# A state-space head and a long-convolution head in one kernel: parameter loads moved to another queue, and a new order of all operations

## The chip, the cores and the metric

The kernel runs on one core of a Trainium2 chip. The time is device microseconds of one launch, the median of the runs shown; the profile is one more execution, recorded by the hardware profiler. The engines are named as in the profile: PE (TensorE matmul) with PEld (its weight loads), DVE (VectorE), ACT (ScalarE), POOL (GpSimd) and SP (SyncE, which here only issues DMAs). Each engine works through its own queue in order.

## What is computed

Two independent heads over one sequence of 2048 positions with 640 channels in bf16; their outputs stand side by side.

```python
def _A_ref(x, Lambda_re, Lambda_im, B_re, B_im, C_re, C_im, log_dt, Dskip):
    Lam = Lambda_re + 1j * Lambda_im
    dt = jnp.exp(log_dt)
    Lam_bar = jnp.exp(dt * Lam)
    B_bar = ((Lam_bar - 1.0) / Lam)[:, None] * (B_re + 1j * B_im)
    Bu = jnp.einsum("bld,pd->blp", x + 0j, B_bar)
    for t in range(L):
        h = Lam_bar[None, :] * h + Bu[:, t, :]
    y = 2.0 * jnp.einsum("blp,dp->bld", hseq, C_re + 1j * C_im).real + x * Dskip
...
def _B_ref(q, k, v, shift_k, ssm_k, ssm_D):
    k_shift = sum over t of 4 taps: k_pad[:, t:t + S, :] * shift_k[:, ks - 1 - t]
    kv = k_shift * v
    y = irfft(rfft(kv, 2 * S) * rfft(ssm_k, 2 * S))[:S]   # per channel
    return q * (y + kv * ssm_D)
...
return jnp.concatenate([a, b], axis=-1)
```

Head A is a linear recurrence with 640 complex states, head B a causal convolution as long as the sequence.

## The kernel before

All operands live in one SBUF arena with named regions; PSUM's eight banks are handed out by number. `build` (line 1008) writes the whole program as a list of 806 operations. An operation has a number (its place in that list), a name, the engines that can do it with a planner's costs, a function that emits its instructions, and the regions that it reads and writes. `Program.depend` (92) derives from the regions which operations must come before which.

The order in which they are emitted, the engine of each and the PSUM bank of each matmul group are one string, `ORDER` (1112): `89V1` is operation 89 on DVE (V) with bank 1, and the other letters are A for ACT, G for POOL, T for PE, S for SP. A small `t` is a PE group whose matmuls are split into narrower pieces that run side by side in the array (`halves`, 585; `s1`, 877 to 883). `Program.emit` (122) walks the string and adds a wait for each dependence between engines. So the string alone sets the order on every engine's queue and the choice of engine where an operation has one: most evictions of PSUM can be done by DVE or ACT, many products of SBUF tiles by DVE or POOL. Where the eviction of a group is on ACT and the DVE form would multiply or add as well, ACT copies and a second operation (`em...`) does the product or sum; where it is on DVE that second one is empty. An `ad` (add) on ACT has PE add the old value through an identity matmul instead (695 to 699).

The stages, with the names that the text uses:

- Warm-ups (0 to 14, lines 513 to 525): matmuls on a zeroed tile while nothing else is there. `setup` and `tables_G` build index tables with iotas on POOL, integer products (`w_q` line 298, `g_q` line 337) and sines on ACT (303, 341).
- Parameters (83 to 147, `params`): three rows of Lambda and dt (84 to 86, line 355) are loaded into a zeroed tile, turned by one matmul (88 t_par, 363) and evicted (89 pv, 365); some thirty small DVE operations lead to the integer phases (105, 385), from there POOL makes multiples (110 fn1 to 114 ph, 393 to 397), ACT their sines (115 al_s, 401), DVE al (116, 403) and the rotation tiles rr (138 to 141, 443).
- B comes in three blocks: the first (154, 155, line 496, by ACT's queue) is turned by PE (156, 158 turn_B, 509) and evicted (157, 159, 511); the second and third (160 to 163, line 500) come by transposing DMAs. x comes in eight tiles (165 to 172 are x0 to x7, line 532), transposing too.
- up2, up1, up0 (198 to 257): B x for four groups of positions at a time, combined by rotations. up2 takes x4 to x7, up1 x2 and x3, up0a x0 and x1 (L566 and L588 to L596 in the profile; evictions L583, L616, L641). 208 up21_0 is the first of them, 220 up0a_0 the first that reads x0 and x1.
- coarse (304 to 324): the recurrence over 128 coarse steps as a scan on DVE, for two halves (307 cs_v0, 316 cs_v1; products L670 to L681). down (325 to 366) spreads it to all positions; project (713 to 805) applies C, adds x Dskip and stores.
- Head B: per block d of 128 channels, k and v are loaded by transposing DMAs (367, 368, 378, 379 and so on, line 815), four taps on DVE or ACT (cm, 837, shown as L205 or L206), sums and the product with v on DVE or POOL (841, 842), a round trip through DRAM (848, 858). All k blocks use one tile, so k1 (378) waits for the last tap of block 0 (374 cm0_0).
- The convolution by two-stage transforms: s1 (L877, L882, evictions L887) and s2 (L901, L914) forward for h (ssm_k) and k, products (pp, pq, py, pz, 925 to 932), r2 (L946, evictions er2 L951) and r1 (L967, er1 L985 or L983) back, for two halves of the channels. 177 addD0 (810) adds ssm_D to h before the first s1.

In the string before, the head of SP's queue is 148, 84, 85, 86, 171, 172, 160, 161, 169, 170, 367, and ACT's is 155, 154, 90.

Of the kernel before, what the change touches and what calls it, by code (L numbers as in the profile page):

```python
# [1092 lines left out]
def plain_order(P):  # L1093
# [16 lines left out]


ORDER = (
# [38 lines left out]
)  # L1151


# [68 lines left out]
```

## Time and profile before

| | us |
|---|---|
| runs shown | 192.4, 192.89, 192.89 |
| their median | 192.89 |
| the profiled execution, as a run | 194.15 |
| its span in the profile | 192.4 |
| PE busy | 179.8 (93%) |
| DVE busy | 162.9 (85%) |
| ACT busy | 141.1 (73%) |
| POOL busy | 73.8 (38%) |

The profile's instructions carry the line of kernel.py that emitted them; `128x1024` is partitions by elements. A queue's DMA issues stand under SPq or ACTq, with the time that the issuing took. The chain of waits is followed back from the last instruction; "issue" is time in which an engine waited for nothing that the profile shows. Operation numbers do not stand in the profile: they follow from the order on each engine.

### The profile page before, as it was taken

Reading aid. Unit: us, or ns where it says so; the run is one execution under the profiler, and the core shown is the slowest. Engines: PE = TensorE matmul, PEld = TensorE weight load, DVE = VectorE, ACT = ScalarE, POOL = GpSimd, SP = SyncE. Lnnn points to the kernel's source line nnn. Section 1 sums busy time; section 2 is a strip of 40 time slices with the busy share of each in tenths; the row PEclk is TensorE's granted clock in tenths of the full one; section 3 lists DMA queues with packets and bytes.
Section 4 is the critical chain, followed back from the end, with each engine's and each line's share of the span. In section 5 each row is a group of like instructions: output and inputs, shape, how many; then the busy total and the mean of one; then the engine's idle time right before and its main releaser. Section 6 shows DMA issues by size and latency. Waiting matters only on the chain.

```text
span 192.4 us, 7725 instructions
## 1 busy us (share of the span) xinstructions
PE 179.8 (93%) x3430; PEld 123.5 (64%) x3431; DVE 162.9 (85%) x226; ACT 141.1 (73%) x176; POOL 73.8 (38%) x60
## 2 busy tenths in 40 slices
PE   7879999999999999879997999999999999989991
PEld 2435555465668666657676766775879877777770
DVE  1837599999789598999989999999999999986841
ACT  2646979999999989999999699983579635581100
POOL 8199999700000000007100578529515020594300
PEclk9999999999999999999999999999999999999999
DMA  4999999999999999939998898209993726447585
GB/s 94 191 172 211 147 203 146 188 108 280 203 146 278 205 162 124 197 67 148 125 135 255 185 134 117 72 3 200 189 234 71 170 72 170 112 135 172 124 184 145
DMA packets 107883, 30.17 MB, mean 157 GB/s; under 512 B 102602, under 2 KB 107210, under 8 KB 107850
## 3 DMA queue, kind: packets, MB, share of 16 engines
q1 hardware_dynamic: 107562, 29.35, 89.5%
q8 instruction: 27, 0.44, 1.0%
q10 hardware_dynamic: 288, 0.33, 0.6%
q14 instruction: 6, 0.05, 0.1%
HBM read 10.99 MB, written 7.86 MB: 98 GB/s over the span
## 4 chain that ended last, share of the span: by engine, by line
PE 59%; DVE 22%; ACT 6%; DMA 5%; SPq 4%; issue 3%; DVEq 0%; ACTq 0%
PE acc L566 23%; PE acc L588 11%; PE acc L592 6%; PE acc L946 6%; PE acc L901 4%; PE acc L596 4%; DVE arena L716 4%; ACT arena L914 3%; DMA arena<-in_A_B_im_dram 2%; DVE arena L914 2%; DVE arena L887 2%; DMA arena<-in_A_Dskip_dram 2%; DVE arena L932 2%; PE acc L967 2%; SPq L532 2%
## 5 line engine op out<-in xcount | busy, mean ns | idle before, releaser
L566 PE MATMUL acc<-arena 128*64 128x512 bf16 x400 | 47.2, 388 | 1.0 <-DMA arena<-in_A_B_im_dram 1.0
L914 ACT CAST arena<-acc 128x960 bf16<-128x960 f32 (+1 forms) x36 | 31.8, 912 | 7.1 <-PE acc L901 6.7
L566 PEld LDWEIGHTS <-arena 128*64 128x64 bf16 x400 | 22.8, 108 | 21.9 <-issue 1.9
L887 ACT CAST arena<-acc 128x1024 bf16<-128x1024 f32 x36 | 34.8, 1068 | 1.4 <-PE acc L877 1.1
L588 PE MATMUL acc<-arena 128*128 128x320 bf16 (+3 forms) x241 | 33.8, 294 | 1.1 <-DVE arena L756 0.8
L588 PEld LDWEIGHTS <-arena 128*128 128x128 bf16 x242 | 21.8, 98 | 10.6 <-DVE arena L756 1.0
L592 PE MATMUL acc<-arena 128*64 128x320 bf16 (+2 forms) x318 | 27.1, 315 | 1.2 <-DVE arena L675 0.8
L901 PE MATMUL acc<-arena 128*64 128x160 bf16 x512 | 22.9, 234 | 0.8 <-ACT arena L914 0.2
L841 POOL TENSOR_TENSOR arena<-arena 128x2048 bf16<-128x2048 bf16 x1 | 4.1, 4066 | 50.7 <-DVE arena L205 50.7
L901 PEld LDWEIGHTS <-arena 128*64 128x64 bf16 x512 | 18.5, 110 | 5.1 <-ACT arena L914 2.2
L841 DVE TENSOR_TENSOR arena<-arena 128x2048 bf16<-128x2048 bf16 x14 | 20.0, 1430 | 2.0 <-ACT arena L206 1.8
L592 PEld LDWEIGHTS <-arena 128*64 128x64 bf16 x318 | 16.9, 110 | 6.3 <-ACT arena L887 1.2
L877 PE MATMUL acc<-arena 128*64 128x128 bf16 x464 | 15.9, 221 | 0.5 <-DVE arena L716 0.2
L951 ACT CAST arena<-acc 128x1024 bf16<-128x1024 f32 x15 | 14.6, 1022 | 2.0 <-PE acc L946 1.9
L877 PEld LDWEIGHTS <-arena 128*64 128x64 bf16 x464 | 13.7, 110 | 3.1 <-ACT arena L887 0.6
L928 POOL TENSOR_TENSOR arena<-arena 128x1280 bf16<-128x1280 bf16 x3 | 8.3, 2769 | 18.3 <-PE acc L877 16.0
L716 DVE TENSOR_TENSOR arena<-acc,arena 128x1024 bf16<-128x1024 f32 (+1 forms) x13 | 14.7, 1154 | 0.2
L205 DVE TENSOR_SCALAR arena<-arena 128x2048 bf16<-128x2048 bf16 (+1 forms) x17 | 13.3, 800 | 0.2
L762 POOL TENSOR_TENSOR arena<-arena 128x640 bf16<-128x640 f32 x3 | 4.4, 1450 | 21.3 <-ACT arena L754 21.3
L946 PE MATMUL acc<-arena 64*128 64x128 bf16 x320 | 11.3, 224 | 1.0 <-issue 0.5
L983 ACT CAST arena<-acc 128x960 bf16<-128x960 f32 (+1 forms) x6 | 4.8, 830 | 10.0 <-PE acc L967 10.0
L946 PEld LDWEIGHTS <-arena 64*128 64x128 bf16 x320 | 10.5, 144 | 2.3 <-issue 1.4
(141 smaller groups left out, 301.9 us busy)
## 6 DMA issues: line engine op xcount, KB each, us to landing
out_dram<-arena SPq DMA_DIRECT2D x31, 160.0 KB, 3.2
arena<-in_B_ssm_k_dram SPq DMA_DIRECT2D x8, 320.0 KB, 5.8
kv_rows<-arena SPq DMA_DIRECT2D x5, 512.0 KB, 3.5
arena<-kv_rows SPq DMA_DIRECT2D x16, 160.0 KB, 5.3
arena<-in_A_x_dram SPq DMA_DIRECT2D x16, 160.0 KB, 3.5
arena<-in_B_q_dram SPq DMA_DIRECT2D x8, 320.0 KB, 5.1
arena<-in_A_B_im_dram ACTq DMA_DIRECT2D x1, 160.0 KB, 2.4
arena<-in_A_B_re_dram ACTq DMA_DIRECT2D x1, 160.0 KB, 2.7
```

Source lines behind the costliest of these rows:

```text
L205: vm = lambda e: lambda out, in_, by: e.tensor_scalar_mul(out=out, in0=in_, scalar1=by)
L566: e.matmul(o[64 * r:64 * r + 64], lhsT=self.BT[j][:, r, d, :], rhs=self.XP[:, d, 2 * q:2 * q + 2], start=(d == 0), stop=(d == 4), skip_gro ...
L588: e.matmul(out, lhsT=lhsT, rhs=rhs, start=start, stop=stop, skip_group_check=True)
L592: e.matmul(out[cs], lhsT=lhsT[:, cs], rhs=rhs, start=start, stop=stop, skip_group_check=True, tile_position=(0, 64 * r))
L716: e.tensor_tensor(out=o, in0=b, in1=o, op=ALU.add)
L841: P.add(f"ca{d}_{j}", tt, lambda e: e.tensor_tensor(out=t1, in0=t1, in1=t2, op=ALU.add), outs=[t1], ins=[t1, t2])
L877: e.matmul(B[64 * b:64 * b + 64, 128 * i:128 * i + 128], lhsT=lh[i], rhs=F[:, b, :], start=True, stop=True, tile_position=(0, 64 * b))
L887: P.add(f"e1{what}{hf}_{u}", {PACT: act(1024), PDVE: dve(1024)}, lambda e, B: c.CP[e](out=out, in_=(B.rearrange("p (l n s k) -> p k s l n" ...
L901: e.matmul(B[64 * s:64 * s + 64, 512 * b + 160 * i:512 * b + 160 * i + 160], lhsT=c.W[:, k, 64 * b:64 * b + 64], rhs=self.AS[hf][:, k, 160 ...
L914: c.CP[e](out=out, in_=b.rearrange("p r (k j n) -> p r k j n", k=n, j=4) if nj > 1 else b.rearrange("p r (k x) -> p r k x", k=n))
L946: e.matmul(B[:, 512 * s + 128 * i:512 * s + 128 * i + 128], lhsT=lh[i][s][r], rhs=rh, start=(r == 0), stop=(r == 1), tile_position=(64 * s ...
L951: P.add(f"er2{hf}_{u}", {PACT: act(1024), PDVE: dve(1024)}, lambda e, B: c.CP[e](out=out, in_=B.rearrange("p (s n b) -> p b s n", s=2, n=4 ...
```

## The change

Only the string is replaced. Everything else, the list of operations with their code included, stays.

```diff
 ORDER = (
-    "148S0 118V0 143G0 83V0 29V0 155A0 0G0 6T6 84S0 7T6 11T4 4T5 30G0 109G0 1T0 16G0 15G0 49G0 58G0 154A0 85S0 86S0 17V0 149G0 88T1 "
-    "89V1 90A0 122V0 34G0 108G0 21G0 23V0 121V0 22V0 117V0 27V0 9T7 24V0 171S0 158T0 159A0 59V0 40V0 153V0 106G0 120V0 61V0 306V0 "
-    "26V0 75G0 107G0 10T7 156T6 91V0 60V0 172S0 92V0 95A0 98V0 65V0 99V0 62V0 67G0 100V0 123V0 42V0 13T7 101V0 41V0 25V0 157A6 "
...
-    "660V0 662V0 629V0 748G0 648V0 562T0 563A0 546T6 547A6 640V0 651V0 749S0 755S0 768S0 769V0 661V0 552T4 553A4 774S0 775V0 770T2 "
-    "771A2 776T6 777V6 675T4 676A4 667T2 668V2 679T0 680A0 683T6 684V6 673T4 674A4 685T2 551G0 558S0 561S0 778G0 766G0 772G0 686A2 "
...
+    "0G0 1T7 143G0 120V0 14T1 30G0 2T4 107G0 16G0 154A0 13T5 6T6 155A0 21G0 119V0 108G0 15G0 83V0 85A0 17V0 12T7 22V0 65V0 67G0 "
+    "24V0 71G0 66V0 86A0 156T4 157V4 10T5 7T1 84A0 11T0 158T5 159A5 4T1 88T2 8T6 89V2 90A0 91V0 92V0 98V0 26V0 118V0 23V0 99V0 27V0 "
+    "100V0 5T4 46G0 95A0 96A0 34G0 36V0 68G0 72G0 148S0 93A0 152A0 172S0 101V0 25V0 9T2 3T0 58G0 59V0 122V0 40V0 60V0 43V0 20A0 "
+    "41V0 42V0 35V0 121V0 102V0 32V0 37V0 123V0 103V0 44V0 61V0 18V0 104V0 28V0 171S0 208T5 209A5 45V0 160S0 117V0 105V0 110G0 "
...
+    "661V0 629V0 550A6 764T2 546T4 547A4 545G0 551G0 659V0 651V0 749S0 755S0 768S0 559S0 774S0 560S0 552T6 553A6 662V0 763V0 640V0 "
+    "775V0 770T0 769V0 771A0 765V2 766V0 776T6 777V6 778G0 561S0 675T4 676A4 772G0 667T2 679T0 680A0 683T6 564V0 668V2 673T4 548G0 "
+    "684V6 767S0 674A4 685T2 686A2 558S0 773S0 779S0 671T0 672V0 786S0 677T6 681T4 800S0 669T2 670V2 554G0 568S0 758T0 757V0 759V0 "
...
 )
```

Read by queue, this gives:

| queue | before | after |
|---|---|---|
| SP, head | 148, 84, 85, 86, x6, x7, 160, 161, x4, x5, k0 | 148, x7, x6, 160, 161, x5, x4, k0 |
| SP, x0 and x1 | v0, k1, x0, x1, v1, pl0 | v0, k1, v1, x1, x0, 260 |
| ACT, head | 155, 154, 90 | 154, 155, 85, 86, 84, 159, 90 |
| PE, head | 5 warm-up groups, 88, 9, 158, 10, 156, 7 groups, 208 | 6 groups, 156, 10, 7, 11, 158, 4, 88, 8, 5, 9, 3, 208 |
| POOL, first table products (68, 72) | after 110 to 112 | before 110 |

ScalarE gives to DVE 132, 134, 157, 199, 205, 219, 255, 265, 332, 348, 467, 544, 563, 670 and 747, and takes from it 135, 207, 209, 213, 247, 249, 374, 471, 550, 556, 590, 644, 655, 678 and 688. DVE gives to POOL 484, 486, 495, 545, 729, 760, 781, 784, 787 and 801, and takes from it 485, 487, 498, 557, 564, 627, 689, 705, 751, 766 and 795 (some of the `em` among these are empty on either side). Of the PE groups in narrow pieces, 33 before, 30 are left, 11 of them new.

64 rows, old and new, of the table ORDER are left out of this document.

## Prediction

> **What bounds the kernel now.** I read the page first, then the busy time in stretches cut where the chain of waits changes engine, then that chain in order of time, then the instructions of the head, of the x loads and of the last stage.
>
> ```profile
> span 192.4 us, 7725 instructions
> PE 179.8 (93%) x3430; PEld 123.5 (64%) x3431; DVE 162.9 (85%) x226; ACT 141.1 (73%) x176; POOL 73.8 (38%) x60
> DMA  4999999999999999939998898209993726447585
> ...
> 12.50:38.40 25.90, 25.90 (x232) 13.78 (x233) 20.69 (x16) 21.47 (x21) 24.59 (x17) 1.00 1.27 178
> 38.40:66.90 28.50, 28.50 (x606) 18.94 (x606) 24.81 (x33) 27.75 (x40) 0.00 (x0) 1.00 1.09 202
> 66.90:165.80 98.90, 93.94 (x2033) 69.92 (x2032) 94.70 (x110) 79.27 (x96) 30.81 (x12) 1.00 0.87 142
> 165.80:188.40 22.60, 21.95 (x516) 17.20 (x516) 16.20 (x21) 7.22 (x8) 11.01 (x7) 1.00 0.59 147
> ```
>
> The columns after the window are its length and the busy time of PE, PEld, DVE, ACT and POOL; the last three are granted clock, share of the DMA engines and GB/s. From 12.5 to 66.9 us PE has no gap at all, and from 38.4 on ACT is nearly as full. From 66.9 to 165.8 DVE is the fullest engine (94.70 of 98.90 us). From 165.8 on PE sets the end again. So no stage has slack to give: the time ahead of 12.5 and the small waits after 66.9 can be won, all else can only be lost.
>
> ```profile
> 1.24 0.49 SPq L355
> ...
> 2.49 1.44 SPq L532
> ...
> 3.98 1.83 SPq L532
> ...
> 5.85 1.79 SPq L500
> ...
> 7.68 4.69 DMA arena<-in_A_B_im_dram
> ...
> 12.50 22.81 PE acc L566 x200
> ```
>
> This is the start of the chain: the three parameter rows (L355) stand ahead of x's tiles 6 and 7 (L532) and of the second block of B (L500) on SP's queue, and PE's steady stream starts when that block lands. The granted clock is 1.00 in every stretch and does not enter.
>
> **The change, part by part.** Every edit is in the order string: the same 806 operations, 3 DMAs moved from SP to ScalarE, 15 evictions and scalings moved from ScalarE to DVE and 15 back, 10 from DVE to POOL and 11 back, and all queues permuted.
>
> *SP's queue.* It loses the three L355 issues: x7 starts at 1.24 where x6 started at 2.49, so what follows is 1.25 us earlier, and the imaginary part of B's block lands at 6.43 + 4.69 = 11.1 instead of 12.4. ScalarE issues the three rows behind its own two loads while it has nothing else to do.
>
> ```profile
> 1.28 3.59 PE L524 MATMUL acc<-arena 128*128 128x512 bf16 x8 [1.28 <-POOL arena L520]
> 5.18 0.17 PE L363 MATMUL acc<-arena 128*128 128x30 bf16 x1 [0.31 <-DMA arena<-in_A_log_dt_dram]
> 5.21 0.38 PE L524 MATMUL acc<-arena 128*128 128x512 bf16 x1
> 5.42 0.44 PE L509 MATMUL acc<-arena 128*128 128x128 bf16 x5
> 6.20 1.47 PE L524 MATMUL acc<-arena 128*128 128x512 bf16 x6
> 9.03 2.45 PE L566 MATMUL acc<-arena 128*64 128x512 bf16 x20
> 9.32 0.17 DVE L385 CAST arena<-arena 128x10 int32<-128x10 f32 x1
> ```
>
> *PE's head.* The first real group (208, up21_0) does not follow x alone: it stands behind the warm-ups. The new queue has nine warm-up matmuls, turn_B, three, turn_B, two, the parameter turn (88), then six. By the rows, with 1.47 / 6 for each later one: 1.28 + 3.59 + 0.38 + 0.44 + 0.74 + 0.44 + 0.49 + 0.17 + 1.47 = 9.0, as now (9.03). It ends at 11.5, when B's block is there, so the second group starts at 11.5 instead of 12.5: **a gain of 1.0 us**, as a start.
>
> The parameter turn goes from 5.18 to 7.4. Behind it DVE has 34 operations up to the phase integers (105, L385); its operations there follow each other by about 0.11 us now, which gives 12 instead of 9.3. POOL's list behind these up to ph (114) I estimate at 9.3 us, so al_s on ScalarE can run from 21.3; ScalarE's own queue reaches it at about 23, after the first evictions and two taps of the k convolution. These 1.7 us cover the delay. If the cover goes, the evictions 201, 215 and 217 right behind al_s are late next, and with them PE's banks.
>
> *The x tiles that come late.* In the new queue x1 and x0 (166, 165) stand behind k1 and v1 (378, 379); now they go between them. And k1 waits for cm0_0 (374), which moves from DVE to ScalarE.
>
> ```profile
> 32.86 2.21 DVE L205 TENSOR_SCALAR arena<-arena 128x2048 bf16<-128x2048 bf16 x1
> 35.10 2.03 SPq L815 DMA_TRANSPOSE arena<-in_B_k_dram  x1
> 37.17 3.25 SPq L532 DMA_TRANSPOSE arena<-in_A_x_dram  x2
> 40.47 4.00 SPq L815 DMA_TRANSPOSE arena<-in_B_v_dram  x1
> ...
> DMA to landing us min/median/max: 3.8/4.8/6.4
> ...
> 49.80 2.43 PE L566 MATMUL acc<-arena 128*64 128x512 bf16 x20
> ```
>
> On ScalarE cm0_0 stands behind the eviction of the last up2 group (207). PE ends that at 11.5 + 9 x 2.28 = 32.0 (22.81 / 10 is the pace of twenty L566 matmuls); behind two table sines that stand ahead of it I put 207's end at 34.2 and cm0_0's, at some 2 us, at 36.2. So k1 goes out at 36.3, v1 at 38.4, x1 at 42.4, x0 at about 44.1 (half of 3.25 for one). The last row but one is the time from issue to landing of the eight x loads. With the median x0 lands at 48.9, with the longest at 50.5. The group that reads both (220, up0a_0) starts at 49.8 now, and would at 48.8 with the gain. I take 6.4, because x1 and x0 stand behind two larger transposes and the DMA engines are full in those slices: 220 at 50.5, so the gain of 1.0 is lost and **0.7 us** with it. Bounds: from 0.9 gained (x0 at 48.9) to 2.0 lost (1.3 us more, for a landing behind v1's data).
>
> *PE from there to cs_v0* (307, now at the end of its gapless stretch) has the same groups, but one s1 group fewer (180 goes ahead of 220) and another no longer split in quarters (192): **-0.15**. ScalarE's list has, by the sum of its rows, 0.7 us more ahead of cs_v0; the 4.4 us that it idles from 12.5 to 38.4 leave room for that.
>
> *DVE's stage.*
>
> ```profile
> 67.41 0.82 DVE L670 TENSOR_TENSOR arena<-acc,arena 128x640 bf16<-128x640 f32 x1 [2.32 <-PE acc L588]
> 74.53 0.42 DVE L641 CAST arena<-acc 128x256 bf16<-128x256 f32 x1 [0.60 <-PE acc L596]
> ...
> L716 DVE TENSOR_TENSOR arena<-acc,arena 128x1024 bf16<-128x1024 f32 x12 | 14.2, 1215 | 0.2
> L928 DVE TENSOR_TENSOR arena<-arena 128x1280 bf16<-128x1280 bf16 x13 | 10.5, 828 | 0.1
> L914 DVE CAST arena<-acc 128x960 bf16<-128x960 f32 x8 | 9.2, 1154 | 0.8 <-PE acc L901 0.4
> L756 DVE TENSOR_TENSOR arena<-acc,arena 128x640 bf16<-128x640 f32 x11 | 8.9, 820 | 2.5 <-PE acc L588 2.0
> ```
>
> DVE waits 2.32 us for cs_v0, so this stage moves with PE. Between cs_v1_m (317) and the last product of the second half 13 operations leave DVE's list and 14 come in. By these means (0.82 us for 640 columns from PSUM or a quarter product, 1.15 for 960, 1.22 for 1024, about 0.45 for the small ones) both sum to 10.8: **0**, bounds 0.7 either way. The wait of 0.60 goes, since its eviction (247) moves to ScalarE; another may come for cs_v1, whose eviction (249) moves too: **-0.3**, between -0.6 and 0.
>
> *The last r2 stage.*
>
> ```profile
> 164.88 0.82 DVE L930 TENSOR_TENSOR arena<-arena 128x1280 bf16<-128x1280 bf16 x1
> 165.62 0.49 DVE L725 TENSOR_TENSOR arena<-arena 128x640 bf16<-128x640 bf16 x1
> 166.24 0.82 DVE L756 TENSOR_TENSOR arena<-acc,arena 128x640 bf16<-128x640 f32 x1
> 167.16 2.35 DVE L951 CAST arena<-acc 128x1024 bf16<-128x1024 f32 x2
> 170.48 2.36 DVE L951 CAST arena<-acc 128x1024 bf16<-128x1024 f32 x2 [0.96 <-PE acc L946]
> 171.79 2.89 PE L588 MATMUL acc<-arena 128*128 128x320 bf16 x20
> ```
>
> Now the last product ends at 165.7 and er21_8 at 169.5, 3.8 us later. The new list puts xd10 (0.4) and ev_C9 (0.8) in between, which now stand ahead; with the overlap of starts that makes 4.8 us. The groups r21_5, r21_7 and r21_1 follow er21_8's bank (1.6 us at their pace), then C8: 6.4 us behind the last product instead of 6.1. **+0.35**; bounds 0 (PE's own pace hides it) to 1.3 (nothing does). Behind C8 the same groups run to the end.
>
> *Sum.* -1.0 + 1.7 - 0.15 - 0.3 + 0.35 = +0.6. The profiled execution took 194.15 us as a run, of which the span is 192.4; all terms are differences within that span, and the median of the runs shown is 192.89, so the forecast is 192.89 + 0.6 = **193.5 us**. About 0.3% (0.58 us) is what a measurement of this kernel can tell from no change.
>
> **The rivals.**
>
> *The head gain stays.* x0 lands by the median: -0.9, -0.15, -0.6, +0.35, together -1.3: 191.6. For it: SP stands idle for some 4 us ahead of k1 in the new queue, so the DMA engines may have emptied. Against it: 6.4 us was needed by loads in this same stretch.
>
> *POOL holds DVE's adds.*
>
> ```profile
> 16.43 2.08 POOL L298 TENSOR_TENSOR arena<-arena 128x1024 int32<-128x1024 int32 x1
> 16.68 1.93 DVE L403 TENSOR_TENSOR arena<-arena 128x80 f32<-128x80 f32 x1
> ```
>
> An 80-column product on DVE took 1.93 us and ended as POOL's table product did. The new list runs two such POOL products (68, 72) at 5 to 9 us, where POOL idles now and DVE has its small parameter operations: up to one product, 1.9 us, which is 0.2 more than al_s's cover. Later POOL's last product (80) can meet addD (177), for which PE waits at 37.5 with nothing before it, and k1's chain moves as well: 193.5 + 0.9 (half a product on average) = 194.4. It decides once POOL's list ends later than 36 us. The Trainium skill, SBUF — State Buffer, Who interferes with whom, says that a DVE instruction with two SBUF inputs and a GpSimd instruction that reads SBUF exclude each other for the whole instruction, which would hold the small products at 7 to 9 us too; no row here shows that at their size.
>
> *Nothing in sum.* The string may not do what it says for the time: PE's head is set by its warm-ups, not by x, and gain, late x and tail cancel to 192.9.
>
> **How the numbers follow.** Forecast 0.39 (own range 193.0 to 194.3), head gain kept 0.33, POOL and later waits 0.15, nothing 0.13. Of the forecast's share 0.32 is slower by over 0.3% and 0.07 within; with 0.14 of POOL's this is slower 0.46, faster 0.34, same 0.20. The range goes from 0.3 under the kept gain, 191.3, to the 2.0 us loss of the x term instead of 0.7 net with the whole tail, 192.89 + 2.0 - 0.15 - 0.3 + 1.3 = 195.7.
>
> **What would show it.** Right: the second up2 group at 11.5; the parameter turn near 7.4; k1 issued after 36; a wait of L566 for x up to about 50.5; cs_v0 near 67.4; more than 4.5 us from the last product to er21_8. Wrong: up0a_0 near 48.9 without a wait (then the time is near 191.6), addD waiting on POOL with s1h0 behind it, or a new gap of over 1 us in DVE between 70 and 165, which none of the terms has.

## The result, and the profile after

The changed kernel is a little faster: its median is 192.38 us (20 runs, 190.55 to 194.75) beside 193.30 us for the kernel before (20 runs, 191.72 to 194.62), a ratio of 0.9933 with a 95% interval of 0.9912 to 0.9955. Two later comparisons of the same two kernels gave 0.9959 [0.9929, 0.9989] and 0.9928 [0.9895, 0.9961]. Over all of its runs the kernel after has a median of 192.36 (44 runs), the kernel before 193.31 (170 runs): 0.95 us. The forecast was 193.5, slower. (A median here is over all runs of a kernel; a ratio leaves out the runs that took over 1.5% more than the kernel's fastest, so the two can differ by some tenths of a per cent.)

The profiled execution took 193.28 us as a run, with a span of 191.5. The page of the kernel after, and the busy time in the stretches of the prediction (length, PE, PEld, DVE, ACT, POOL, granted clock, DMA share, GB/s):

```profile
span 191.5 us, 7710 instructions
PE 181.0 (94%) x3425; PEld 123.9 (65%) x3425; DVE 157.3 (82%) x226; ACT 143.5 (75%) x176; POOL 71.9 (38%) x60
```

```profile
12.50:38.40 25.90, 25.80 (x286) 13.94 (x282) 15.47 (x14) 23.72 (x24) 22.39 (x20) 1.00 1.17 157
38.40:66.90 28.50, 27.12 (x530) 18.21 (x526) 23.28 (x32) 26.61 (x36) 0.00 (x0) 1.00 1.09 194
66.90:165.80 98.90, 94.43 (x2043) 69.27 (x2040) 96.09 (x114) 80.02 (x97) 28.70 (x11) 1.00 0.82 145
165.80:188.40 22.60, 22.41 (x521) 17.41 (x518) 15.47 (x19) 8.88 (x10) 12.31 (x8) 1.00 0.67 167
```

The bounds are the same ones: PE to 66.9 us, DVE to 165.8, PE to the end. New is a hole in PE between 38.4 and 66.9 (27.12 of 28.50 where the kernel before had 28.50). The start of the chain of waits and PE's and SP's timelines of the kernel after show the head and that hole:

```profile
3.04 1.83 SPq L532
4.92 1.79 SPq L500
6.75 1.75 SPq L500
```

```profile
7.08 0.18 PE L363 MATMUL acc<-arena 128*128 128x30 bf16 x1
...
8.50 2.45 PE L566 MATMUL acc<-arena 128*64 128x512 bf16 x20
11.25 2.04 PE L566 MATMUL acc<-arena 128*64 128x512 bf16 x16 [0.30 <-DMA arena<-in_A_B_im_dram]
...
50.98 2.47 PE L566 MATMUL acc<-arena 128*64 128x512 bf16 x20 [1.34 <-ACT arena L341]
```

```profile
36.07 2.13 SPq L815 DMA_TRANSPOSE arena<-in_B_k_dram  x1
38.25 3.38 SPq L815 DMA_TRANSPOSE arena<-in_B_v_dram  x1
41.67 3.37 SPq L532 DMA_TRANSPOSE arena<-in_A_x_dram  x2
```

The second up2 group starts at 11.2 instead of 12.5, the parameter turn (L363) stands at 7.1, k1 goes out at 36.07, and up0a_0 waits 1.34 us. The view puts that wait down to a sine on ACT (L341), but this group does not read it. Of the two x loads of the last row the view of line 532 says:

```profile
L532 SPq DMA_TRANSPOSE arena<-in_A_x_dram x2: 1407/1664/1922, 41.7 to 43.1; - x2
...
DMA to landing us min/median/max: 4.5/6.1/7.7
```

x0, issued at 43.12, took the longest of these: it landed at 50.85, and the group started 0.1 us later. In another execution of the same kernel (the run e15 below) ACT's sines stand where they stood, PE starts before they end, and x0 took 5.3 us:

```profile
48.48 2.22 ACT L341 ACTIVATE arena<-arena 128x1024 bf16<-128x1024 int32 x2
...
49.45 2.48 PE L566 MATMUL acc<-arena 128*64 128x512 bf16 x20
```

```profile
DMA to landing us min/median/max: 4.5/4.9/5.3
```

So every sign that the prediction named for being right is in the first profile (cs_v0 at 67.77, and 4.87 us from the last product to er21_8), and still the kernel is faster. Here and below a PE group starts with its first weight load, up to 0.25 us ahead of its first matmul. C0 to C15 are the groups of project, `st_A0` to `st_A15` their stores; s2k0_19, s1h1_3 and r10_16 are single groups of s2, s1 and r1. PE's last group, C13, starts only 0.1 us earlier than before (186.55 against 186.65); the other 0.8 us of the spans' difference lies behind it, where nothing but stores runs. SP's queue at the end, before and after:

```profile
179.96 0.35 SPq L766 DMA_DIRECT2D out_dram<-arena  x1
180.69 0.35 SPq L740 DMA_DIRECT2D out_dram<-arena  x1
181.13 1.66 SPq L724 DMA_DIRECT2D arena<-in_A_x_dram  x1
182.84 4.72 SPq L1001 DMA_DIRECT2D out_dram<-arena  x6
187.66 1.02 SPq L766 DMA_DIRECT2D out_dram<-arena  x2
188.86 0.33 SPq L740 DMA_DIRECT2D out_dram<-arena  x1
```

```profile
178.57 0.34 SPq L724 DMA_DIRECT2D arena<-in_A_x_dram  x1
179.01 3.33 SPq L1001 DMA_DIRECT2D out_dram<-arena  x4
182.39 0.49 SPq L766 DMA_DIRECT2D out_dram<-arena  x1
...
187.81 0.35 SPq L766 DMA_DIRECT2D out_dram<-arena  x1
188.77 0.35 SPq L740 DMA_DIRECT2D out_dram<-arena  x1
```

Before, two of part B's first four stores of the second half (L1001) stand behind st_A15 and st_A13, which wait for their evictions, and behind a load that takes 1.66 us to issue; six stores of 160 KB then go out in one row. After, all four go out at 179.0. The windows of before and of after (the last two columns are DMA share and GB/s):

```profile
180.00:184.00 4.00, 4.00 (x149) 3.16 (x149) 2.77 (x4) 0.69 (x1) 1.39 (x1) 1.00 0.57 146
...
188.00:193.00 5.00, 0.30 (x3) 0.00 (x0) 0.49 (x1) 0.00 (x0) 0.00 (x0) 0.98 0.47 122
```

```profile
180.00:184.00 4.00, 4.00 (x120) 2.93 (x118) 3.53 (x5) 0.96 (x1) 1.40 (x1) 1.00 0.88 197
...
188.00:193.00 5.00, 0.21 (x2) 0.00 (x0) 0.49 (x1) 0.00 (x0) 0.00 (x0) 0.74 0.34 91
```

The DMA engines are half idle where the kernel after uses them, and that work is still in flight at the end: the last store lands 2.62 us after its issue before and 1.78 after.

One execution of a kernel differs from the next by up to 1 us in its parts, so the account below is made from all profiles of the runs that follow, stage by stage, between starts of PE groups that have the same work ahead of them in both orders (the median, in brackets the range and the number of executions that run this stage in that order, single moved operations aside; e2, which its waits put 7 us back, is left out behind cs_v0):

| stage, us | old order | new order | forecast |
|---|---|---|---|
| start to the third up2 group (up21_4) | 14.46 (14.14 to 14.64, 7) | 13.57 (13.25 to 14.03, 12) | -1.0 |
| from there to cs_v0 | 52.34 (52.30 to 52.77, 7) | 52.84 (52.42 to 54.43, 8) | +1.55 |
| the same, x0 and x1 between k1 and v1 | | 52.46 (52.45 to 52.62, 3) | |
| cs_v0 to C8 | 104.34 (103.67 to 104.94, 4) | 103.99 (103.70 to 106.06, 12) | +0.05 |
| of it, r10_16 to C8 | 12.55 (12.33 to 12.91, 5) | 11.90 (11.89 to 12.04, 11) | +0.35 |
| C8 to C13, PE's last group | 14.86 (14.86 to 15.07, 6) | 14.86 (13) | 0 |
| C13 to the end | 5.72 (5.18 to 6.03, 5) | 5.26 (4.76 to 6.73, 12) | 0 |

The medians' differences add up to -0.9 + 0.5 - 0.35 - 0.5 = -1.25, the means' to -0.8 + 0.65 + 0 - 0.3 = -0.45; the times say -0.95.

### The profile page after: what moved, and what is told of

The parts are those of the page before. It is cut to its first block, busy times and chain, and to the rows that moved or that the text cites. A ratio compares the mean times of both kernels' runs of the same rounds, so it can differ in the third digit from the quotient of the medians.

```text
span 191.5 us, 7710 instructions
## 1 busy us (share of the span) xinstructions
PE 181.0 (94%) x3425; PEld 123.9 (65%) x3425; DVE 157.3 (82%) x226; ACT 143.5 (75%) x176; POOL 71.9 (38%) x60
## 4 chain that ended last, share of the span: by engine, by line
PE 55%; ACT 18%; DVE 11%; SPq 6%; issue 5%; DMA 4%; ACTq 0%; DVEq 0%
PE acc L588 17%; PE acc L566 12%; PE acc L901 6%; PE acc L946 6%; ACT arena L887 5%; PE acc L592 4%; DMA arena<-in_B_k_dram 4%; DVE arena L716 4%; SPq L532 4%; ACT arena L914 3%; PE acc L877 3%; ACT arena L206 3%; PE acc L967 3%; PE acc L596 3%; ACT arena L341 2%
## 5 line engine op out<-in xcount | busy, mean ns | idle before, releaser
L588 PE MATMUL acc<-arena 128*128 128x320 bf16 (+3 forms) x290 | 42.1, 299 | 0.2 <-issue 0.2
L914 ACT CAST arena<-acc 128x960 bf16<-128x960 f32 (+1 forms) x39 | 34.0, 902 | 7.7 <-PE acc L901 7.3
L566 PEld LDWEIGHTS <-arena 128*64 128x64 bf16 x400 | 23.7, 108 | 22.3 <-issue 1.7
L588 PEld LDWEIGHTS <-arena 128*128 128x128 bf16 x290 | 26.3, 98 | 12.4 <-ACT arena L914 0.8
L841 POOL TENSOR_TENSOR arena<-arena 128x2048 bf16<-128x2048 bf16 x1 | 4.1, 4075 | 53.5 <-DVE arena L205 53.5
L901 PEld LDWEIGHTS <-arena 128*64 128x64 bf16 x512 | 18.2, 109 | 6.0 <-ACT arena L914 3.1
L841 DVE TENSOR_TENSOR arena<-arena 128x2048 bf16<-128x2048 bf16 x14 | 17.8, 1275 | 3.6 <-ACT arena L206 3.5
L592 PE MATMUL acc<-arena 128*64 128x320 bf16 (+2 forms) x216 | 18.6, 312 | 0.9 <-DVE arena L675 0.6
L716 DVE TENSOR_TENSOR arena<-acc,arena 128x1024 bf16<-128x1024 f32 (+1 forms) x15 | 16.1, 1109 | 0.1
L877 PEld LDWEIGHTS <-arena 128*64 128x64 bf16 x416 | 12.7, 110 | 4.2 <-ACT arena L887 2.0
L205 DVE TENSOR_SCALAR arena<-arena 128x2048 bf16<-128x2048 bf16 (+1 forms) x17 | 11.3, 680 | 4.5 <-DMA arena<-in_B_k_dram 4.3
L983 ACT CAST arena<-acc 128x960 bf16<-128x960 f32 (+1 forms) x7 | 5.8, 845 | 11.8 <-PE acc L967 9.9
L592 PEld LDWEIGHTS <-arena 128*64 128x64 bf16 x216 | 11.5, 110 | 4.2 <-ACT arena L887 1.0
L756 DVE TENSOR_TENSOR arena<-acc,arena 128x640 bf16<-128x640 f32 x12 | 9.8, 820 | 4.2 <-PE acc L588 3.5
L990 POOL TENSOR_TENSOR arena<-arena 128x960 bf16<-128x960 bf16 (+1 forms) x5 | 8.8, 1769 | 11.4 <-ACT arena L983 11.4
L946 PE MATMUL acc<-arena 64*128 64x128 bf16 x320 | 11.2, 225 | 0.3 <-DVE arena L756 0.3
```

The lines of the kernel that those rows point to most:

```text
L205: vm = lambda e: lambda out, in_, by: e.tensor_scalar_mul(out=out, in0=in_, scalar1=by)
L566: e.matmul(o[64 * r:64 * r + 64], lhsT=self.BT[j][:, r, d, :], rhs=self.XP[:, d, 2 * q:2 * q + 2], start=(d == 0), stop=(d == 4), skip_gro ...
L588: e.matmul(out, lhsT=lhsT, rhs=rhs, start=start, stop=stop, skip_group_check=True)
L592: e.matmul(out[cs], lhsT=lhsT[:, cs], rhs=rhs, start=start, stop=stop, skip_group_check=True, tile_position=(0, 64 * r))
L716: e.tensor_tensor(out=o, in0=b, in1=o, op=ALU.add)
L841: P.add(f"ca{d}_{j}", tt, lambda e: e.tensor_tensor(out=t1, in0=t1, in1=t2, op=ALU.add), outs=[t1], ins=[t1, t2])
```

## The experiments

All edits are in the order string unless said otherwise. In the diffs, `SP:` is a part of SP's queue. Medians with the number of runs, and the ratio to the kernel before on the same chip.

**Three splices.** Because both strings hold the same 806 operations, a head of one can be followed by the rest of the other.

e1, the new head:

```diff
-old[0:806]
+new[0:300] + what is left, as in old
```

> The new order up to and with cs_v0 (its first 300 operations), the old order for the rest. Theory A (the new head loses time because x's tiles 1 and 0 come late, and what was won lies behind the head): PE waits about 1.3 us for x ahead of up0a_0, cs_v0 starts 0.9 us later than before (near 67.8), and that reaches the end: 193.3 + 0.9 = 194.2. Rival B (the head's earlier start is what the end shows): 192.4. Rival C (the old middle takes up what the head loses, since DVE sets the end there): 193.3.

193.94 (12), 1.0026 [0.9995, 1.0056]. cs_v0 at 66.27, with 0.41 us of waiting ahead of up0a_0: the head does not lose the 0.9 of theory A. But from cs_v0 to s2k0_19, 87 us into the kernel, it takes 20.90 us where both whole orders take 19.9: the seam costs 1.0.

e2, the new middle:

```diff
-old[0:806]
+old[0:301] + new up to 700 operations + what is left, as in old
```

> The old order up to cs_v0, the new one for the operations between (some 400, to about 165 us), the old one from there. Theory A: the middle gives back what the head loses, so alone it makes the kernel some 0.9 us faster: 192.4. Rival B: the middle is neutral: 193.3. Rival C (moved evictions put waits on DVE that the new head covers): 194.

199.81 (6), 1.0347 [1.0304, 1.0390]: no theory. From cs_v0 to s2k0_19 it takes 23.1 us where both whole orders take 19.9, and at the other end C10 waits for C9's eviction, which the new order has behind the last product, while the old order gives C10 the same bank:

```profile
165.99 1.25 PE L588 MATMUL acc<-arena 128*128 128x320 bf16 x4 [2.69 <-DVE arena L756]
```

e3, the new tail:

```diff
-old[0:806]
+old[0:700] + what is left, as in new
```

> The old order up to about 165 us, the new one for its last 106 operations. Theory A (the last stores of the new order reach SP's queue sooner, so that the last one has fewer transfers in flight beside it): the last product (C13) ends where it did, within 0.4 us, and the last store lands under 2 us after its issue instead of 2.6: 193.3 - 0.8 = 192.5. Rival B (the end of the profiled executions differs by chance): 193.3, the last store as before. Rival C (the wait for er21_8 behind the last product is paid at the end): 193.6.

194.37 (12), 1.0070 [1.0039, 1.0102], over all three theories. At its seam PE waits 1.23 us ahead of r10_22, and the last store needs 2.7 us. None of the three splices can be read as a part of the change: each seam brings a wait of 1 us or more that neither order has.

**Where x's tiles 0 and 1 stand.** e4 issues them ahead of k1, e6 between k1 and v1 as the kernel before does, all else as after; e12 and e16 are repeats of e6, e5 and e15 of the kernel after.

```diff
-SP: 368 378 379 166 165 260
+SP: 368 166 165 378 379 260      (e4)
+SP: 368 378 165 166 379 260      (e6, e12, e16)
```

> The kernel after, with x's tiles 1 and 0 issued ahead of k1 and v1 instead of behind them. Theory A: x0 lands before 45, the 1.34 us ahead of up0a_0 go, cs_v0 starts near 66.5; all carried to the end this is 192.4 - 1.3 = 191.1. Rival B (the stage of DVE behind it takes up what PE wins, since the k and v transfers are now 3 us later): cs_v0 early, but the time within 0.4 of 192.4. Rival C (k1 at 39 instead of 36 delays the gated product, and DVE waits for it): slower than 192.8.

194.13 (12), 1.0020 [0.9982, 1.0058], with a spread of 191.84 to 196.38: rival C as a time. Its profile is of the fastest of these runs (span 190.1, cs_v0 at 65.94); why the others are slower it cannot show.

> The kernel after, unchanged, beside the other three on this chip. Every theory expects a median within 0.4 of 192.4 and a ratio near 0.993. The second profile says which differences of the first belong to the order and which to one execution. Theory A (the order decides): x0 lands 6.4 to 7.8 us after its issue, up0a_0 waits for it up to between 49.4 and 51, and the last store lands under 2 us after its issue, which is within 0.6 us of the end of C13's eviction. Rival B (the first profile was one of many): one of the two is not there again.

192.91 (12), 0.9959 [0.9929, 0.9989]. x0 took 5.2 us and landed at 48.83, and there is no wait ahead of up0a_0: rival B. The last store took 2.1 us, a little over what theory A has. cs_v0 came at 67.31 all the same: from up21_4 on this execution took 53.75 us, and what held it was not x but a POOL product (under DVE's stage below).

> The kernel after, with x's tiles 0 and 1 between k1 and v1, as the kernel before has them. Theory A (the late x costs time that reaches the end): no wait ahead of up0a_0, cs_v0 0.4 to 1.3 us earlier than in the kernel after, median 191.4 to 192.0. Rival B (DVE's stage behind cs_v0 takes it up, or v1's later landing gives it back): cs_v0 early, median 192.4 within 0.4. Rival C (as with x ahead of k1, where the median came out at 194.1): slower than 193.

192.28 (12), 0.9936 [0.9903, 0.9969], cs_v0 at 66.48: rival B.

> The kernel after with x's tiles 0 and 1 between k1 and v1, a second time. Theory A (the late x costs some tenths in most executions): under 192.5, with no wait ahead of up0a_0 and cs_v0 near 66.5. Rival B (the late x costs nothing that reaches the end): 192.4 to 192.9, as the kernel after has it.

192.00 (12), 0.9935 [0.9900, 0.9969], cs_v0 at 66.56: theory A.

> The kernel after, unchanged, beside the next run. Every theory: 192.3 to 192.9; the time from r10_16 to C8 is 11.9 us and from C8 to the end 19.6 to 20.1.

192.18 (12), 0.9928 [0.9895, 0.9961], cs_v0 at 66.25. From C8 to the end it took 20.5 us, outside of what was expected.

> The kernel after with x's tiles 0 and 1 between k1 and v1, a third time. Theory A (the late x costs some tenths in most executions): 0.3 to 0.7 us under the run beside it, as in the first two comparisons (192.28 to 192.91 and 192.0 to 192.6). Rival B (it costs nothing that reaches the end): within 0.2 of it.

192.16 (10), 0.9943 [0.9904, 0.9983], cs_v0 at 66.12: within 0.02 of the run beside it, rival B. Together 192.12 (34 runs) against 192.36 (44); the means differ by 0.28 with a standard error of 0.2. The late x costs a few tenths at most, and whether it costs anything in the time is not settled. The version with x between k1 and v1 beats the kernel before in all three comparisons, the kernel after in none that can be told from chance.

**Old head, new rest.** e7:

```diff
-new[0:806]
+old[0:301] + what is left, as in new
```

> The old order up to and with cs_v0 (301 operations), the new one for all that follows: the mirror of the run with the new head alone, which took 193.9 against 193.35. Theory A (the new head costs 0.6 of itself, the gain lies behind it): 191.8. Rival B (the new order behind it needs what its head prepares, since the middle alone ran into waits): over 193.3, with a new wait of over 1 us between 67 and 165. Rival C (the head decides nothing): 192.4.

194.18 (12), 1.0056 [1.0029, 1.0084]. Rival B as a time; but the waits, 0.99 and 0.76, stand directly behind cs_v0, at the seam, and from there to s2k0_19 it needs 21.55 us instead of 19.9.

**Two stores on ScalarE's queue.** e8, the kernel before:

```diff
-785S0 ... 799S0
+785A0 ... 799A0
```

> The kernel before, with the stores of C12 and C14 (st_A12, st_A14) issued by ScalarE, which is idle by then, instead of standing behind six other stores on SP's queue. Theory A (that queue, full at the end, is what sets the end of the kernel before): st_A12 goes out when its eviction ends, near 186.1 instead of 187.7, the last store lands under 2 us after its issue instead of 2.6, and the kernel gains 0.8: 192.5. Rival B (the landing is set by the bytes in flight, whoever issues them): 193.3. Rival C (the execution's spread is larger than this): no difference of 0.4 in the medians either way.

193.16 (12), 0.9997 [0.9972, 1.0021]. st_A12 went out at 186.04 instead of 187.66, and the last store still took 2.55 us. A full queue on SP is not what holds the end; rival B.

**The row of D.** e9, the kernel before:

```diff
-SP: 261 259 429 428 430 431 151 713 87 718
+SP: 261 259 713 87 429 428 430 431 151 718
```

> The kernel before, with the first row load of x (ld_r0) and the row of D (ld_Dr) issued ahead of the second half's four h loads, where SP's queue is empty, instead of behind them. Both profiles of the old middle that have the wait show DVE idle 0.6 to 0.75 us for this row ahead of xd0, and PE 0.85 to 1.0 us ahead of the next group of its bank (near 101). Theory A (that vanished wait is one of the terms of the gain): the PE wait at 101 is gone, the groups from s1h1_3 on start 0.8 us earlier, median 192.5 to 192.8. Rival B (later stages, where DVE and the banks set the pace, take it up): the wait gone, but median within 0.3 of 193.35. Rival C (the h loads, now 1 us later, delay addD1): slower than 193.7.

The rows in the kernel before, and in e9:

```profile
100.31 0.49 DVE L725 TENSOR_TENSOR arena<-arena 128x640 bf16<-128x640 bf16 x1 [0.59 <-DMA arena<-in_A_Dskip_dram]
...
101.82 0.60 PE L588 MATMUL acc<-arena 128*128 128x512 bf16 x2 [0.85 <-DVE arena L756]
```

```profile
99.76 0.47 DVE L725 TENSOR_TENSOR arena<-arena 128x640 bf16<-128x640 bf16 x1
...
101.24 0.61 PE L588 MATMUL acc<-arena 128*128 128x512 bf16 x2 [0.16 <-DVE arena L756]
```

193.11 (12), 0.9999 [0.9966, 1.0033]: rival B. The wait is gone and the time is not. e3 and e14 run this stretch in the old order unedited, without the wait (14.9 us from s2k0_19 to s1h1_3 instead of 15.6): it belongs to some executions, not to the order.

**The old tail behind the new order.** e10:

```diff
-new[0:806]
+new[0:747] + what is left, as in old
```

> The kernel after up to and with C8 (172 us), the old order for the last 59 operations: in its tail six stores of part B's second half stand in a row ahead of st_A12 and st_A14, and these two and st_A13 are the last three transfers. Theory A (fewer bytes in flight at the end are 0.5 to 0.8 us of the gain): C13 within 0.3 us of the kernel after, the time from C13's start to the end of the span 5.6 to 6.3 us instead of 4.8 to 5.3, median 192.6 + 0.6 = 193.2. Rival B (chance): 4.8 to 5.3 us again, median 192.6.

193.24 (12), 0.9982 [0.9941, 1.0023]: the time of theory A, but the stretch of rival B. From C13 to the end it took 5.18 us, with C13 itself 0.2 later behind C8; and PE had lost 1.2 us at 98.8 by a late load of h, which is not in the edit.

**The parameter rows back on SP.** e11, the kernel after:

```diff
-SP: 148 172 171 160 161       ACT: 154 155 85 86 84
+SP: 148 84 85 86 172 171 160 161       ACT: 154 155
```

> The kernel after, with the three parameter rows back on SP's queue ahead of x7. Theory A (the head's gain reaches the end): the second up2 group starts 0.7 to 1.2 us later than in the kernel after, cs_v0 as much later, median 192.6 + 0.8 = 193.4. Rival B (the head's gain is lost to x's late tiles or to DVE's stage anyway): the second group later, cs_v0 at most 0.4 later, median within 0.4 of 192.6.

```profile
12.48 0.88 PE L566 MATMUL acc<-arena 128*64 128x512 bf16 x6 [1.23 <-DMA arena<-in_A_B_im_dram]
```

193.01 (12), 0.9948 [0.9907, 0.9989]. The second group is back at 12.5, so the gain of the head is the three rows and nothing else. cs_v0 comes at 68.90, but 1.26 us of that are a wait inside up0a_0 at 52 us that no other execution has and that the view puts down to nothing ("issue"). The median is 0.65 over the pooled one of the kernel after; the intervals overlap.

**C9's eviction and xd10 ahead of the last product again.** e13 and, unchanged, e17, from the kernel after:

```diff
-DVE: 763 640 775 769 765 766
+DVE: 763 765 766 769 640 775
```

> The kernel after, with C9's eviction and xd10 ahead of DVE's last product again (as in the kernel before) and nothing else. Theory A (the move is a gain: PE waits for the last product in the old order, at 165.5, and no longer in the new): PE waits again ahead of r21, the time from r10_16's start to C8's is 12.3 to 12.9 us instead of 11.9, median 192.6 + 0.5 = 193.1. Rival B (the forecast's step: the move costs 0.35, so undoing it gains): 11.6 us or the same, median 192.2. Rival C (no difference, PE's own pace hides it): 11.9, median 192.6.

192.92 (12), 0.9956 [0.9922, 0.9990]. In the kernel before, in the kernel after, and in e13 (DVE's L932 at 164.2 and 164.5 are the last product of the latter two; the former's is at 164.88, L930):

```profile
165.85 3.67 PE L946 MATMUL acc<-arena 64*128 64x128 bf16 x108 [0.36 <-ACT arena L754]
...
170.03 1.83 PE L946 MATMUL acc<-arena 64*128 64x128 bf16 x52 [0.51 <-issue]
```

```profile
164.25 0.82 DVE L932 TENSOR_TENSOR arena<-arena 128x1280 bf16<-128x1280 bf16 x1
...
165.79 1.54 DVE L756 TENSOR_TENSOR arena<-acc,arena 128x640 bf16<-128x640 f32 x2
166.33 5.43 PE L946 MATMUL acc<-arena 64*128 64x128 bf16 x160
```

```profile
163.33 0.83 DVE L756 TENSOR_TENSOR arena<-acc,arena 128x640 bf16<-128x640 f32 x1
...
164.47 0.82 DVE L932 TENSOR_TENSOR arena<-arena 128x1280 bf16<-128x1280 bf16 x1
...
165.35 5.45 PE L946 MATMUL acc<-arena 64*128 64x128 bf16 x160
```

r10_16 to C8 took 12.02 us in e13 and 12.04 in e17, not 12.3 and not 11.6: rival C, for this stage.

> The kernel after with C9's eviction and xd10 ahead of the last product, a second time. Theory A (where a long issue of SP falls among the last stores is a property of one execution): from C13's start to the end 4.7 to 5.7 us, as the kernel after has it, median 192.2 to 192.7. Rival B (this order causes it: st_A9 and what follows it on SP's queue meet another moment): 6.3 us or more again, one of the four stores ahead of st_A15 takes over 2 us to issue, median 192.9 or more.

193.16 (12), 0.9985 [0.9952, 1.0019]. From C13 to the end 6.73 us in e13 and 5.02 in e17: theory A, one execution's property; the median is rival B's. This execution lost 1.5 us elsewhere, where a late load of h holds addD1 (810) and PE with it:

```profile
99.13 0.52 DVE L810 TENSOR_TENSOR arena<-arena 128x80 bf16<-128x80 bf16 x1 [1.25 <-DMA arena<-in_B_ssm_k_dram]
...
99.71 0.45 PE L882 MATMUL acc<-arena 64*64 64x64 bf16 x32 [1.53 <-DVE arena L810]
```

As a time this edit is not neutral: the 24 runs of e13 and e17 have a median of 192.99 against 192.36, and their mean is 0.6 higher (95% interval 0.2 to 1.0); e13 is 0.7 over e15, which ran beside it. That is near theory A's 193.1 in e13, while the stage that theory A named loses only 0.1. Where the rest goes the two profiles do not show: one was long at the end and the other at 98 us.

**Fewer bytes at the end.** e14 leaves the last four stores of part B's second half out of the kernel before, e18 out of the kernel after (part of the output is not written):

```diff
-lambda e, s=s, dst=dst: e.dma_start(out=dst, in_=s)
+lambda e, s=s, dst=dst: (hf, b0) == (1, 0) or e.dma_start(out=dst, in_=s)
```

> The kernel before without the last four stores of part B's second half (640 KB of output are not written; the order is unchanged). Theory A (the bytes that these stores have in flight set the landing of the last store): st_A12 goes out at once, the last store lands under 2 us after its issue, from C8's start to the end of the span 19.6 to 20.0 us instead of 20.5 to 20.8, median 193.35 - 0.8 = 192.6. Rival B (the last store needs its 2.6 us whatever is beside it): 20.5 us, median 193.3.

192.22 (7), 0.9929 [0.9895, 0.9964]; C13 to the end 4.84 us instead of 5.72, and under all five executions that write these bytes in the old order: theory A. SP's rows and the window at the end of e14:

```profile
185.31 1.94 SPq L766 DMA_DIRECT2D out_dram<-arena  x2
187.83 0.33 SPq L740 DMA_DIRECT2D out_dram<-arena  x1
```

```profile
188.00:193.00 5.00, 0.00 (x0) 0.00 (x0) 0.00 (x0) 0.00 (x0) 0.00 (x0) 0.78 0.10 33
```

> The kernel after without the last four stores of part B's second half (640 KB of output are not written). Theory A (bytes in flight set the landing of the last store in both orders, and the new order has fewer of them by then): from C13's start to the end 4.6 to 4.9 us, 0.2 to 0.5 less than the kernel after's mean, median 192.4 - 0.35 = 192.05; the kernel before gained 0.85 in that stretch by the same. Rival B (the new order's tail is as full as the old one): 0.8 us gained again, median 191.5.

192.40 (12), 0.9956 [0.9921, 0.9991]; C13 to the end 4.82 us. Both kernels come to the same 4.83 without these bytes, from 5.72 and from 5.3 (the mean of the kernel after's 4.95, 5.25 and 5.61). That is theory A's stretch; but e11 and e4, which write all bytes behind the same tail, took 4.76 and 4.81, and the median shows no gain. So for the new order nothing is shown.

## Why the prediction was wrong

**The baseline.** The forecast was built on a median of 192.89 out of three runs; 170 runs have 193.31. This hid a part of the miss: as a difference the forecast was +0.6, and -0.95 came.

**The head's gain: right.** Forecast -1.0, found -0.9, and e11 shows that moving the three rows is all of it.

**The late x: this step failed.** The working took 6.4 us from issue to landing "because x1 and x0 stand behind two larger transposes and the DMA engines are full", and lost 1.7. In the eight executions of this head x0 was on its way for 4.82, 5.15, 5.24, 5.27, 5.30, 6.64, 6.80 and 7.72 us, and it was issued at 42.4 to 43.6, not at 44.1. The first profile, with 7.72, is the worst of them; there the 1.3 us of waiting are real. PE waited for x in three of the eight (1.34, 0.69 and 0.41 us) and in the other five not at all. The median loss from up21_4 to cs_v0 is 0.5, and e6, e12 and e16 are 0.4 better; but not all of that is x, since e5 lost at least 0.7 there to POOL. The range given (0.9 gained to 2.0 lost) held it; the choice inside it was wrong. The row with the median, which gave the first rival's 191.6, was the better one: that rival's difference, -1.3, is nearer to -0.95 than the forecast's. In part that is luck: it had the wrong sign for the last r2 stage, nothing for the end, and a gain in DVE's stage that did not come.

**DVE's stage: right in sum, for other reasons.** From cs_v0 to r10_16 the medians of the two orders differ by 0.4 us (91.7 old, 92.1 new), and executions of the new one by 2.2 (91.8 to 94.0). Late loads make that: the row of D in the old order, h of the second half in the new (addD1 waited 0.90, 1.25 and 0.78 us for it in e10, e17 and e18). The wait of 0.60 that was to go counts for nothing beside them.

**POOL and DVE: the rival's mechanism came, in two executions and at another place.** No POOL product held addD0, where the rival looked for it: addD0 (L810) took 0.53 us at 36.30 with no POOL product beside it, where before it took 2.64 beside one. But at 23.6 us a sum on DVE (L841) and a product on POOL (L298) come up together. In the first profile of the kernel after, DVE begins first and POOL's product takes the longer for it; in e5 both begin within 0.01 us, and DVE is held:

```profile
23.57 1.23 DVE L841 TENSOR_TENSOR arena<-arena 128x2048 bf16<-128x2048 bf16 x1 [0.30 <-ACT arena L206]
...
23.66 2.89 POOL L298 TENSOR_TENSOR arena<-arena 128x1024 int32<-128x1024 int32 x1
```

```profile
23.64 2.98 DVE L841 TENSOR_TENSOR arena<-arena 128x2048 bf16<-128x2048 bf16 x1 [0.39 <-ACT arena L206]
...
23.65 1.89 POOL L298 TENSOR_TENSOR arena<-arena 128x1024 int32<-128x1024 int32 x1
...
39.81 2.45 PE L566 MATMUL acc<-arena 128*64 128x512 bf16 x20 [0.72 <-ACT arena L616]
```

In e5 the next products on DVE are late and held too (L443 takes 3.49 us instead of 1.49), a tap on ACT waits for them, ACT's eviction (L616) comes 0.8 us later, and PE waits 0.72 us for it. Of the thirteen executions in which POOL, DVE and ACT run the new head, e5 and e11 went this way; POOL's list ended by 35.3 us in all of them, so the 36 us that the rival named as its condition did not decide. That the shared port does this is stated in the Trainium skill, SBUF — State Buffer, Who interferes with whom, for a DVE instruction with two SBUF inputs; these traces agree.

**The last r2 stage: wrong sign.** The forecast priced what was moved behind the last product (er21_8 4.87 us behind it, as expected) and took the product's own end as fixed. But the product ended 5.3 us behind r10_16's start instead of 6.8, and PE's waits in r2 are gone: the 0.36 ahead of it, which all five executions of the old order have (0.57 in e1), and the 0.51, which e8, e9 and e1 do not have. By the medians the stage gained 0.65 where 0.35 was to be lost. The 1.3 us of work that no longer stand ahead of the product are not the reason: in e13 and e17 they stand there again, the product ends 6.6 us behind r10_16's start, and still PE waits under 0.1 us and the stage loses only 0.1. What takes the wait away was not tried.

**The end: a term that was missing.** "Behind C8 the same groups run to the end" is true of PE, and the kernel does not end with PE. The order of the stores changes how many bytes are in flight when the last one is issued. e14 shows that in the old order these bytes set the landing, with 0.9 us; in the new order e18 does not show it. All six executions that write everything with the old tail (e2 is one) have a DMA share of 0.50 to 0.61 in the four microseconds that begin 6.65 us ahead of C13's start, all twelve with the new tail 0.74 to 0.93. That share is the order's; what comes of it at the end varies, from 4.8 to 6.7 us, so the half microsecond between the medians is not shown to come from it alone: e3 and e7 have the new tail and 5.9 and 6.3 us.

What stays open: the parts add up to something between -0.45 and -1.25, and the splices, which were to separate them, brought waits of their own. Why e13's and e17's edit costs 0.6 us is open too.

## What to carry to other kernels

Follow the sum to the last store's landing and not to the last matmul: in the kernel before, the bytes still in flight there cost 0.9 us, so try letting stores that are ready go out ahead of those that wait for an eviction. When a load is moved, take the median of its like from issue to landing and keep the longest for the range, and have a second profile before a wait in one of them is believed. Where DVE and POOL come up within 0.1 us of each other, either can be the one that waits. A searched order is one piece: where two are joined, the seam costs more than the parts are worth.

## What the runs showed of the hardware

In the last 20 us of these kernels the shortest issue on SP took 0.32 to 0.34 us, in every execution, and the longest 2.15. In the first profile of the kernel after the three issues of over 1 us behind 175 us (at 175.87, 180.72 and 185.03) each begin within 0.3 us of one of the 16-KB packets that the trace lists as instruction loads (175.87, 180.58, 184.79); in e13 the one of 2.15 us at 179.39 follows such a packet at 179.09. Over all twenty profiles there are 49 issues of over 1 us in the last 20 us; all begin within 0.8 us of the start of such a packet and 43 within 0.4, while of the 324 shorter ones only 23 are within 0.4. This is a coincidence in time, not shown as a cause. The Trainium skill, Runtime: NRT & Kernel Launch, Instruction fetch mechanics, has blocks of this size and calls their cost mostly hidden; if the long issues are theirs, it was not hidden here.

The last store, where its landing is recorded, never landed sooner than 1.59 us behind its issue (e11), with or without others beside it.

Two executions whose SP queues agree to 0.15 us from 166 to 180 us (the kernel after and e7) ended 1.3 us apart; the first issue in which they differ took 0.71 us in the one and 2.11 in the other.
